# Fourier mixing and a gated MLP on one core: three reads of the first group issued by GpSimd, the last row's numbers of a piece of w_in by a transfer, and the last chunk's epilogue in smaller steps

## The chip, the cores and the metric

The kernel runs on one core of a Trainium2 chip. A core has five instruction streams: PE (matrix products; its weight loads are listed apart as PEld), DVE (VectorE), ACT (ScalarE), POOL (GpSimd) and SP (SyncE, which here only issues transfers). Each runs its own instructions in order and waits for the others by semaphores. Transfers are issued on the queues of SP, ACT or GpSimd. The metric is the device time of one execution in microseconds (us); lower is better.

## The reference

x has 8 batches of 3008 rows of 256 numbers, all float32. The reference takes the real part of a two-dimensional Fourier transform of each batch, and passes the 24064 rows through an MLP with a hard-swish gate:

```
X = real(fft(fft(x, axis=1), axis=2))      # (8, 3008, 256) -> (24064, 256)
h = X @ w_in                               # (24064, 2048)
g = h * clip(h + 3, 0, 6) / 6
out = g @ w_out                            # (24064, 256)
```

## The kernel before

**The mathematics.** The transform over 3008 = 47 x 64 rows is done in two stages of products with tables (`stage1`, `stage1_first` for the 47, `stage2` for the 64). The transform over the 256 columns is folded into w_in: the table C (256 x 256) times a piece of w_in gives the tile W1, so one product does both (`fold_w_in`, L664). The last of the 256 table rows is dealt with apart: its numbers, one for each of the 2048 columns of w_in, stand in row 127 of the second half of W1, and are needed spread over the partitions in the tile WN (128 x 16, one column for each block of 128 columns of w_in). DVE multiplies a column of WN with a row of data and adds it to a product (`s`, L401, in `activate`). The second matrix product of the MLP takes 7 block products in place of 8 (`mlp2`, L473), whose sums and differences are made in an epilogue (`finish`; for the last chunk of all `finish_final`, L513).

**Tiles and order.** Batches go in four pairs; a pair has 12 chunks of output frequencies in 6 groups of two; a chunk has 8 steps `fc`. A step takes blocks fc and fc + 8 of the 16 column blocks. In step fc of a chunk, `mlp1` makes two products u and v of W1 with the tile q of the group, `activate` makes the gate, `combine` three sums on GpSimd, and `mlp2` adds seven products into four PSUM tiles `acc`. The whole order is written out by hand: the tile framework places the semaphores, but moves nothing. The loop at L924 runs over the steps, with the next pair's stage 1 put beside them by due step. The first eight steps have an order of their own (`first_steps`, `second_steps`), since the weights are still being prepared.

**The start.** The first pair's x is read by GpSimd's queue, stage 1 runs column by column, and its result z is stored to DRAM by SP's queue (`zd`, L285). It comes back transposed as the tile g of the first group: `load_g(first, 0)` (L305), four reads on SP, two halves (`h`, L314) for two batches (`b`), which wait for the last store. Meanwhile the weights arrive in 16 pieces of 512 KB by GpSimd's queue (`load_w`, L577). Pieces 0 and 1 are the first two of w_in and 2 and 3 the first two of w_out. `see` (L743) is a copy of one column by GpSimd of the first half of g; it stands ahead of `load_w` for pieces 4 to 7 (L773), so these are issued only when the first half of g is there. Each piece is taken apart into exponent and mantissa and joined again (`exponent_a`, `exponent_b`, `exponent_c` at L605 to L625, `mantissa`, `join`). Then come `fold_w_in(0)` and `fold_w_in(1)` (L787, L791), `stage2` of the first group's first half (L797), and chunk 0's first products.

**fold_w_in.** Eight products on PE (16 instructions) into a PSUM tile, a copy of it into W1 by ACT (L684), and the numbers for WN. For piece 0 they go by two transfers on SP (L691), each from row 127 of W1, 128 numbers of 4 bytes, one to each partition. For piece 1 (`spread_by_pe=True`) PE multiplies instead the piece's own columns with the table's last row, four products of one column (L682, tile `pw`), and ACT copies the two columns into WN (L686). For later pieces a transfer is issued for the first of the two columns of each piece, and the second column of an even piece waits in the list `rest` until the next piece. The first step uses WN columns 0 (piece 0) and 8 (piece 1), the second step columns 1 and 9.

**The end.** In the last step of the last chunk `mlp2` makes its seven products in the order 0, 1, 2, 3, 4, 6, 5. After product 0 ACT copies it, scaled, into the tile e (L490). The other products are used from PSUM by DVE in `finish_final`: `add_product` adds a product to a sum (L522), `turn_both` transposes both halves of one output side together in 32 x 32 blocks (L526) and sends it in six stores (`send`, L555), which alternate between SP's queue and ACT's; in the second group of six the last one goes on SP. Four sums lead to the first side, `rn[:, 0]`; then two more, and one instruction for both halves of the second side (L537).

Of the kernel before, what the change touches and what calls it, by code (L numbers as in the profile page):

```python
# [7 lines left out]
F32 = mybir.dt.float32  # L8
# [5 lines left out]
AL = mybir.AluOpType  # L14
# [34 lines left out]
WS = 2.0 ** 20  # L49
# [9 lines left out]
def kernel(  # L59
# [10 lines left out]
    nc = tc.nc  # L70
    P = nc.NUM_PARTITIONS
    B, S, D = x.shape
    FF = moe_w_in.shape[1]
    NFC = FF // P
    NF = NFC // 2
# [12 lines left out]
    TB = KC * N2  # L88
    NH = N2 // 2 + 1
    NG = NCK // 2  # L90
    DH = 32
# [13 lines left out]
    ps_h = ctx.enter_context(tc.tile_pool(name="ps_h", bufs=3, space=PSUM))  # L105
# [14 lines left out]
    C = consts.tile([P, 2, D], F32, name="C")  # L120
    W1 = consts.tile([P, 2, FF], F32, name="W1")
    WN = consts.tile([P, NFC], F32, name="WN")
# [182 lines left out]
    def load_g(pr, gr):  # L305
        g = gpool.tile([P, 2 * KK, D + 1], F32, tag="g", name="g")
        gb = [g[b * N2:(b + 1) * N2] for b in range(2)]
        for b in range(2):
            zd = pr.zd[b, gr] if pr.p > 0 else pr.zd[gr, b]
            zd = zd.rearrange("k c n d -> (c n) k d")  # L310
            if pr.p > 0 or gr > 0:
                nc.sync.dma_start(out=gb[b][:, :, 0:D if pr.p > 0 else D + 1], in_=zd)

        for h in range(2 if pr.p + gr == 0 else 0):  # L314
            ks = slice(h * KK, (h + 1) * KK)
            for b in range(2):
                nc.sync.dma_start(out=gb[b][:, ks], in_=pr.zd[gr, b, ks].rearrange("k c n d -> (c n) k d"))
        for b in range(2) if pr.p > 0 else ():
            nc.sync.dma_start(out=gb[b][:, :, D], in_=pr.zq[gr, :, :, :, b].rearrange("k c n -> (c n) k"))
        pr.g[gr] = g  # L320
# [152 lines left out]
    def mlp2(ch, fc):  # L473
        a = ch.a.pop(fc)[:].rearrange("p m f n -> p (m f) n")[:, :, 0:ch.n]
        c = ch.c.pop(fc)
        moving = [a[:, 0], a[:, 1], a[:, 3], c[:, 0], c[:, 1], c[:, 2], c[:, 3]]
        order = list(enumerate(moving))
        if ch.final and fc == NF - 1:

            order[5:] = order[:4:-1]  # L480
        for i, mv in order:

            if fc == 0 and i % 2 == 0:
                ch.acc[i // 2] = ps_a.tile([P, 2, TB], F32, tag="acc", name="acc")
            nc.tensor.matmul(ch.acc[i // 2][:, i % 2, 0:ch.n], G[:, i, fc, :], mv,  # L485
                             start=(fc == 0 and i % 2 == 0), stop=(fc == NF - 1), skip_group_check=True)
            if ch.final:
                if fc == NF - 1 and i == 0:
                    ch.e = epool.tile([P, 8, TB], F32, tag="e", name="e")
                    nc.scalar.mul(ch.e[:, 0, 0:ch.n], ch.acc[0][:, 0, 0:ch.n], 1.0 / WS)  # L490
                continue
            if fc == NF - 1 and (i % 2 == 1 or i == 6):
                if i == 1:
                    ch.e = epool.tile([P, 8, TB], F32, tag="e", name="e")
                k = 2 * (i // 2)
                nc.scalar.mul(ch.e[:, k:i + 1, 0:ch.n], ch.acc[i // 2][:, 0:i + 1 - k, 0:ch.n], 1.0 / WS)  # L496

    def finish(ch):
# [14 lines left out]
    def finish_final(ch):  # L513
        n = ch.n
        e = ch.e[:, 0, 0:n]
        w = epool.tile([P, 3, TB], F32, tag="w", bufs=1, name="w")
        ch.r = epool.tile([P, 2, 2, TB], F32, tag="r", name="r")
        wn, rn = w[:, :, 0:n], ch.r[:, :, :, 0:n]
        os = [epool.tile([P, TB // DH, 2, DH], F32, tag="o", name="o") for m in range(2)]

        def add_product(out, i, in1, sign=1.0):
            nc.vector.scalar_tensor_tensor(out, ch.acc[i // 2][:, i % 2, 0:n], sign / WS, in1,  # L522
                                           op0=AL.mult, op1=AL.add)

        def turn_both(m):
            nc.vector.transpose(os[m][:, 0:n // DH].rearrange("p j h e -> p h j e"),  # L526
                                rn[:, m].rearrange("p h (j i) -> p h j i", i=DH))
            send(ch, os[m], m)

        add_product(rn[:, 0, 0], 1, e)  # L530
        add_product(wn[:, 0], 3, e)
        add_product(wn[:, 2], 6, wn[:, 0])
        add_product(rn[:, 0, 1], 5, wn[:, 2], -1.0)
        turn_both(0)
        add_product(wn[:, 1], 4, e)
        add_product(wn[:, 0], 5, wn[:, 1], -1.0)
        nc.vector.scalar_tensor_tensor(rn[:, 1], ch.acc[1][:, :, 0:n], 1.0 / WS, wn[:, 0:1].to_broadcast([P, 2, n]),  # L537
                                       op0=AL.mult, op1=AL.add)
        turn_both(1)

    def store(ch, m):
        o = epool.tile([P, TB // DH, 2, DH], F32, tag="o", name="o")
# [4 lines left out]
    def turn(ch, o, m, h):  # L547
        n = ch.n
        nc.vector.transpose(o[:, 0:n // DH, h], ch.r[:, m, h, 0:n].rearrange("p (j i) -> p j i", i=DH))  # L549

    def send(ch, o, m):

        queues = [nc.sync, nc.scalar, nc.sync, nc.scalar, nc.sync, (nc.scalar, nc.sync)[m]]
        for j, (bj, k1) in enumerate(ch.blocks[m]):
            (queues[j] if ch.final else nc.sync).dma_start(out=out_k[ch.pr.p, k1, bj], in_=o[:, j].rearrange("p h e -> p (h e)"))  # L555
# [105 lines left out]

    rest = []

    def fold_w_in(j, spread_by_pe=False):  # L664

        _, n, k = PIECES[j]
        nb = WB // 2
        cs = slice(in_column(n, k), in_column(n, k) + nb)
        wi = w.pop(PIECES[j]).rearrange("p (i f) -> p i f", i=2)

        ps = bank([P, 2, nb], "wps") if starting[0] else spare[k]
        for blk in range(2):
            for i in range(2):
                nc.tensor.matmul(ps[:, blk], C[:, i, blk * P:(blk + 1) * P], wi[:, i], start=(i == 0), stop=(i == 1))  # L674
        fs = range(cs.start // P, cs.stop // P)

        pw = None
        if spread_by_pe:
            pw = ps_h.tile([P, nb // P], F32, tag="uv", name="pw")
            for f in range(2):  # L680
                for i in range(2):
                    nc.tensor.matmul(pw[:, f:f + 1], wi[:, i, f * P:(f + 1) * P], C[:, i, D - 1:D],  # L682
                                     start=(i == 0), stop=(i == 1))
        nc.scalar.copy(W1[:, :, cs], ps[:])  # L684
        if pw is not None:
            nc.scalar.copy(WN[:, fs[0]:fs[-1] + 1], pw[:])  # L686
            return

        wait = [] if k or j == 0 else fs[1:]
        for f in [fs[0], *rest, *(() if wait else fs[1:])]:  # L690
            nc.sync.dma_start(out=WN[:, f:f + 1], in_=W1[P - 1:P, 1, f * P:(f + 1) * P])  # L691
        rest[:] = wait
# [95 lines left out]
    head_b(2)  # L788
    exponent_b(2)
    exponent_a(3)  # L790
    fold_w_in(1, spread_by_pe=True)  # L791
    head_b(3)
    exponent_b(3)
    tail(2)
# [54 lines left out]
    epool = None  # L849
# [7 lines left out]
    uv = mlp1_products(*chunk(0))  # L857
# [184 lines left out]
```

## Time and profile before

| | |
|---|---|
| device time, four runs | 1941.18, 1942.77, 1944.06, 1944.3 us (median 1943.42) |
| the profiled execution: device time, span | 1945.75 us, 1943.8 us |
| share of full clock granted to PE, mean | 0.997 |
| DVE, ACT, POOL busy | 1437.8, 680.6, 1417.6 us |
| read from and written to HBM | 57.57 MB, 37.32 MB |
| first product that is part of the second matrix product (L465) | 52.04 us |
| last product ends | 1934.4 us |

The span runs from the first instruction to the last of the profiled execution; the device time has also what lies around it. All times in the views count from the start of the span. In a line of the timeline the columns are the start, the length, the engine (a q after it: its queue of issued transfers), the line in the code, the operation, the tile written and those read, the number of merged instructions, and in brackets how long the engine had been idle and what ended that. A line of the chain has start, length, and the work or the transfer that the chain went through; "issue" is time in which the engine waited for nothing that the profile shows.

### The profile page before, as it was taken

The numbers are of one execution on the slowest core, as the hardware profiler recorded it, in microseconds if no ns is written. First come the engines' busy times: TensorE is split into PE (matmuls) and PEld (weight loads), VectorE is DVE, ScalarE is ACT, GpSimd is POOL, SyncE is SP. The second block draws the span as 40 slices with busy tenths as digits, with TensorE's granted clock in tenths as the row PEclk, the third lists the DMA queues.
The fourth block names the chain that finished last, engine by engine and source line by source line (L and its number), as shares of the span: only waits on it lengthen the run. The fifth ranks groups of instructions, "written<-read, shape, count | busy, mean of one in ns | idle before, by whom it ended". The sixth has DMA issues, their size and how long they took to land.

```text
span 1943.8 us, 27874 instructions
## 1 busy us (share of the span) xinstructions
PE 1926.7 (99%) x9228; PEld 1656.9 (85%) x9228; DVE 1437.8 (74%) x2777; ACT 680.6 (35%) x1162; POOL 1417.6 (73%) x1620
## 2 busy tenths in 40 slices
PE   9999999999999999999999999999999999999997
PEld 4578888888988888888898888888899888888887
DVE  6877777777777777777787777777778777777776
ACT  5633333333333333333333333333333333333332
POOL 4178888887678877787678877878666667666664
PEclk9999999999999999999999999999999999999999
DMA  8521222211111222111111221222110101101000
GB/s 225 189 72 47 74 49 55 55 44 31 39 33 50 57 74 55 44 50 32 37 36 46 55 55 44 50 53 52 35 28 20 28 17 28 34 12 28 21 18 20
DMA packets 149854, 96.70 MB, mean 50 GB/s; under 512 B 118687, under 2 KB 132131, under 8 KB 149710
## 3 DMA queue, kind: packets, MB, share of 16 engines
q1 hardware_dynamic: 138378, 58.09, 12.4%
q0 software_dynamic: 10672, 36.67, 6.5%
q8 instruction: 72, 1.18, 0.2%
q14 instruction: 72, 0.59, 0.1%
q10 hardware_dynamic: 660, 0.16, 0.0%
HBM read 57.57 MB, written 37.32 MB: 49 GB/s over the span
## 4 chain that ended last, share of the span: by engine, by line
PE 94%; DVE 2%; DMA 1%; ACT 1%; issue 1%; POOL 0%; DVEq 0%; ACTq 0%
PE acc L485 56%; PE v L392 16%; PE u L392 16%; PE ps L335 2%; PE acc L465 1%; PE ps L223 1%; DMA xt<-in_x_dram,IX 1%; DVE a L441 1%; DVE s L401 0%; ACT t L438 0%; DVE u L422 0%; PE spare L674 0%; PE ps L278 0%; DVE o L549 0%; DMA WN<-W 0%
## 5 line engine op out<-in xcount | busy, mean ns | idle before, releaser
L455 POOL TENSOR_TENSOR c<-a 128x512 f32<-128x512 f32 (+1 forms) x375 | 469.0, 1251 | 360.9 <-PE acc L485 291.9
L485 PE MATMUL acc<-c,G 128*128 128x256 f32 (+1 forms) x3008 | 696.9, 374 | 0.0
L438 ACT ACTIVATE t<-u,half 128x512 f32<-128x512 f32 (+1 forms) x384 | 260.8, 679 | 1141.3 <-DVE u L411 1056.0
L485 PEld LDWEIGHTS acc<-c,G 128*128 128x128 f32 x3008 | 565.4, 190 | 71.1
L401 DVE SCALAR_TENSOR_TENSOR s<-qn,WN,u 128x256 f32<-128x256 f32 (+1 forms) x768 | 330.5, 472 | 333.4 <-PE u L392 331.2
L485 PE MATMUL acc<-a,G 128*128 128x256 f32 (+1 forms) x2256 | 541.5, 375 | 0.5 <-ACT e L490 0.5
L485 PEld LDWEIGHTS acc<-a,G 128*128 128x128 f32 x2256 | 421.4, 190 | 71.9 <-issue 17.6
L392 PE MATMUL v<-q,W 127*128 127x256 f32 (+1 forms) x1536 | 389.3, 375 | 3.1 <-DVE a L441 3.1
L392 PE MATMUL u<-q,W 128*128 128x256 f32 (+1 forms) x1536 | 388.0, 375 | 0.3 <-ACT q L338 0.3
L441 DVE SCALAR_TENSOR_TENSOR a<-t,u 128x512 f32<-128x512 f32 (+2 forms) x448 | 263.9, 601 | 102.2 <-ACT t L438 98.5
L392 PEld LDWEIGHTS v<-q,W 127*128 127x128 f32 x1536 | 287.9, 190 | 43.8 <-DVE a L441 3.9
L392 PEld LDWEIGHTS u<-q,W 128*128 128x128 f32 x1536 | 285.7, 190 | 37.0 <-issue 1.9
L455 POOL TENSOR_TENSOR c<-a,c 128x256 f32<-128x256 f32 (+1 forms) x375 | 269.1, 717 | 29.4
L455 POOL TENSOR_TENSOR c<-c,a 128x256 f32<-128x256 f32 (+1 forms) x375 | 269.0, 717 | 29.4
L411 DVE TENSOR_TENSOR u<-s,v 128x512 f32<-128x512 f32 x352 | 245.0, 696 | 37.7 <-DVE s L401 1.4
L441 DVE SCALAR_TENSOR_TENSOR a<-t,v 128x512 f32<-128x512 f32 (+1 forms) x480 | 263.9, 567 | 0.3 <-ACT t L438 0.2
L438 ACT ACTIVATE t<-v,half 128x512 f32<-128x512 f32 (+1 forms) x384 | 260.7, 679 | 0.4 <-issue 0.2
L413 DVE TENSOR_TENSOR v<-v,s 128x512 f32<-128x512 f32 x352 | 244.0, 693 | 0.0
L455 POOL TENSOR_TENSOR r<-w,e 128x256 f32<-128x256 f32 (+1 forms) x92 | 88.8, 986 | 3.6
L496 ACT ACTIVATE e<-acc 128x512 f32<-128x512 f32 (+2 forms) x184 | 83.4, 545 | 0.0
L549 DVE STREAM_TRANSPOSE o<-r 128x256 f32<-128x256 f32 (+1 forms) x188 | 71.1, 417 | 0.1
L455 POOL TENSOR_TENSOR w<-w,e 128x512 f32<-128x512 f32 (+1 forms) x46 | 57.6, 1251 | 3.6
(113 smaller groups left out, 778.0 us busy)
## 6 DMA issues: line engine op xcount, KB each, us to landing
out_dram<-o SPq DMA_DIRECT2D x747, 32.0 KB
zd<-z SPq DMA_DIRECT2D x48, 192.0 KB
g<-zd SPq DMA_DIRECT2D x36, 256.0 KB
xt<-in_x_dram POOLq DMA_DIRECT2D x21, 256.0 KB, 3.7
qn<-qd SPq DMA_DIRECT2D x19, 256.0 KB
st<-in_moe_w_in_dram POOLq DMA_DIRECT2D x8, 512.0 KB, 4.6
st<-in_moe_w_out_dram POOLq DMA_DIRECT2D x8, 512.0 KB
xt<-in_x_dram POOLq DMA_DIRECT2D x17, 192.0 KB, 3.9
```

The costliest lines, as they stand in the source:

```text
L223: nc.tensor.matmul(ps[b][h * PB:(h + 1) * PB, 0:n], F[rows(b), 0:PB], y[rows(b), 2 * h:2 * h + n], start=True, stop=not last, skip_group_c ...
L335: nc.tensor.matmul(ps[:, blk, u * P:n].rearrange("p (b k) -> p b k", b=2), g[:, kk, blk * (P + 1):blk * (P + 1) + P], T[:, :, gr, blk, kk, ...
L392: nc.tensor.matmul(ps[:, i, 0:nq], W1[r, blk, f * P:(f + 1) * P], q[r, blk, of:of + nq], start=True, stop=True)
L401: nc.vector.scalar_tensor_tensor(s[:, i, 0:nq], qn[:, of:of + nq], WN[:, f:f + 1], u[:, i, 0:nq], op0=AL.mult, op1=AL.add)
L411: nc.vector.tensor_tensor(u[:], s[:], v[:], op=AL.add)
L413: nc.vector.tensor_tensor(v[:], v[:], s[:], op=AL.subtract)
L438: nc.scalar.activation(t, h, AF.Relu, bias=half[:], scale=scale)
L441: nc.vector.scalar_tensor_tensor(dst, t, 1.0, h, op0=AL.min, op1=AL.mult)
L455: (eng or nc.gpsimd).tensor_tensor(out, in0, in1, op=AL.add)
L485: nc.tensor.matmul(ch.acc[i // 2][:, i % 2, 0:ch.n], G[:, i, fc, :], mv, start=(fc == 0 and i % 2 == 0), stop=(fc == NF - 1), skip_group_c ...
L496: nc.scalar.mul(ch.e[:, k:i + 1, 0:ch.n], ch.acc[i // 2][:, 0:i + 1 - k, 0:ch.n], 1.0 / WS)
L549: nc.vector.transpose(o[:, 0:n // DH, h], ch.r[:, m, h, 0:n].rearrange("p (j i) -> p j i", i=DH))
```

## The change

Three parts, in one diff. In `load_g(first, 0)` the first of the four reads stays on SP, and the other three are issued by GpSimd. `fold_w_in` loses the way by PE: for piece 0 one transfer is issued and the other column waits in `rest`; for piece 1 three transfers follow its copy into W1: column 8, then column 1 (from `rest`), then column 9. In the last step of the last chunk ACT's copy of product 0 comes after product 1 in the order of the program, and `finish_final` transposes each half as soon as it is there (`turn`, L547, unchanged), with four smaller transposes in place of two, and two sums of one half in place of one instruction for both.

```
--- before.py
+++ after.py
@@ -314,7 +314,9 @@
         for h in range(2 if pr.p + gr == 0 else 0):
             ks = slice(h * KK, (h + 1) * KK)
             for b in range(2):
-                nc.sync.dma_start(out=gb[b][:, ks], in_=pr.zd[gr, b, ks].rearrange("k c n d -> (c n) k d"))
+
+                (nc.sync if h + b == 0 else nc.gpsimd).dma_start(
+                    out=gb[b][:, ks], in_=pr.zd[gr, b, ks].rearrange("k c n d -> (c n) k d"))
         for b in range(2) if pr.p > 0 else ():
             nc.sync.dma_start(out=gb[b][:, :, D], in_=pr.zq[gr, :, :, :, b].rearrange("k c n -> (c n) k"))
         pr.g[gr] = g
@@ -484,15 +486,14 @@
                 ch.acc[i // 2] = ps_a.tile([P, 2, TB], F32, tag="acc", name="acc")
             nc.tensor.matmul(ch.acc[i // 2][:, i % 2, 0:ch.n], G[:, i, fc, :], mv,
                              start=(fc == 0 and i % 2 == 0), stop=(fc == NF - 1), skip_group_check=True)
-            if ch.final:
-                if fc == NF - 1 and i == 0:
-                    ch.e = epool.tile([P, 8, TB], F32, tag="e", name="e")
-                    nc.scalar.mul(ch.e[:, 0, 0:ch.n], ch.acc[0][:, 0, 0:ch.n], 1.0 / WS)
-                continue
             if fc == NF - 1 and (i % 2 == 1 or i == 6):
                 if i == 1:
                     ch.e = epool.tile([P, 8, TB], F32, tag="e", name="e")
                 k = 2 * (i // 2)
+                if ch.final:
+                    if k == 0:
+                        nc.scalar.mul(ch.e[:, 0, 0:ch.n], ch.acc[0][:, 0, 0:ch.n], 1.0 / WS)
+                    continue
                 nc.scalar.mul(ch.e[:, k:i + 1, 0:ch.n], ch.acc[i // 2][:, 0:i + 1 - k, 0:ch.n], 1.0 / WS)
 
     def finish(ch):
@@ -522,21 +523,19 @@
             nc.vector.scalar_tensor_tensor(out, ch.acc[i // 2][:, i % 2, 0:n], sign / WS, in1,
                                            op0=AL.mult, op1=AL.add)
 
-        def turn_both(m):
-            nc.vector.transpose(os[m][:, 0:n // DH].rearrange("p j h e -> p h j e"),
-                                rn[:, m].rearrange("p h (j i) -> p h j i", i=DH))
-            send(ch, os[m], m)
-
         add_product(rn[:, 0, 0], 1, e)
+        turn(ch, os[0], 0, 0)
         add_product(wn[:, 0], 3, e)
         add_product(wn[:, 2], 6, wn[:, 0])
         add_product(rn[:, 0, 1], 5, wn[:, 2], -1.0)
-        turn_both(0)
+        turn(ch, os[0], 0, 1)
+        send(ch, os[0], 0)
         add_product(wn[:, 1], 4, e)
         add_product(wn[:, 0], 5, wn[:, 1], -1.0)
-        nc.vector.scalar_tensor_tensor(rn[:, 1], ch.acc[1][:, :, 0:n], 1.0 / WS, wn[:, 0:1].to_broadcast([P, 2, n]),
-                                       op0=AL.mult, op1=AL.add)
-        turn_both(1)
+        for h in range(2):
+            add_product(rn[:, 1, h], 2 + h, wn[:, 0])
+            turn(ch, os[1], 1, h)
+        send(ch, os[1], 1)
 
     def store(ch, m):
         o = epool.tile([P, TB // DH, 2, DH], F32, tag="o", name="o")
@@ -661,7 +660,7 @@
 
     rest = []
 
-    def fold_w_in(j, spread_by_pe=False):
+    def fold_w_in(j):
 
         _, n, k = PIECES[j]
         nb = WB // 2
@@ -673,20 +672,9 @@
             for i in range(2):
                 nc.tensor.matmul(ps[:, blk], C[:, i, blk * P:(blk + 1) * P], wi[:, i], start=(i == 0), stop=(i == 1))
         fs = range(cs.start // P, cs.stop // P)
-
-        pw = None
-        if spread_by_pe:
-            pw = ps_h.tile([P, nb // P], F32, tag="uv", name="pw")
-            for f in range(2):
-                for i in range(2):
-                    nc.tensor.matmul(pw[:, f:f + 1], wi[:, i, f * P:(f + 1) * P], C[:, i, D - 1:D],
-                                     start=(i == 0), stop=(i == 1))
         nc.scalar.copy(W1[:, :, cs], ps[:])
-        if pw is not None:
-            nc.scalar.copy(WN[:, fs[0]:fs[-1] + 1], pw[:])
-            return
-
-        wait = [] if k or j == 0 else fs[1:]
+
+        wait = [] if k else fs[1:]
         for f in [fs[0], *rest, *(() if wait else fs[1:])]:
             nc.sync.dma_start(out=WN[:, f:f + 1], in_=W1[P - 1:P, 1, f * P:(f + 1) * P])
         rest[:] = wait
@@ -788,7 +776,7 @@
     head_b(2)
     exponent_b(2)
     exponent_a(3)
-    fold_w_in(1, spread_by_pe=True)
+    fold_w_in(1)
     head_b(3)
     exponent_b(3)
     tail(2)
```

## The prediction

> **What bounds the kernel now.** I read the page first, then the chain of waits of the first 110 us, the timelines there engine by engine, the busy time by stretches, and the timeline of the last 20 us. The page settles where not to look:
>
> ```profile
> PE 1926.7 (99%) x9228; PEld 1656.9 (85%) x9228; DVE 1437.8 (74%) x2777; ACT 680.6 (35%) x1162; POOL 1417.6 (73%) x1620
> PE 94%; DVE 2%; DMA 1%; ACT 1%; issue 1%; POOL 0%; DVEq 0%; ACTq 0%
> ```
>
> PE is busy for 99% of the span and makes 94% of the chain. The diff touches no instruction between the second piece of w_in and the last chunk, so it can act in two places: before PE becomes gapless (about 76 us), where a shift of the start moves everything behind it one for one, and after the last product. The chain at the start:
>
> ```profile
> 44.05 0.80 PE pw L682 x8
> 44.85 0.02 issue
> 44.87 0.16 ACT WN L686
> 45.03 1.05 ACT ex L625 x2
> 46.08 0.48 ACT q L338
> ...
> 61.99 4.98 DMA WN<-W
> 66.98 0.02 issue
> 67.00 0.49 DVE s L401
> ```
>
> The reader is to see that PE's `pw`, its copy and ACT's next three instructions were on the chain, and that much later a `WN` transfer of one tile is waited for 4.98 us. GpSimd's timeline beside it:
>
> ```profile
> 44.70 0.62 POOL L744 COPY seen<-g 128x1 f32<-128x1 f32 x1 [14.65 <-DMA g<-zd]
> 45.26 1.44 POOL L585 DMA_DIRECT2D st<-in_moe_w_in_dram  x2
> ...
> 61.53 0.79 POOL L585 DMA_DIRECT2D st<-in_moe_w_in_dram  x1 [5.59 <-ACT PM L605]
> ```
>
> `see` holds GpSimd until the half-tiles of `g` are there (44.70); only then do the 512 KB reads of the next weight pieces start (45.26). The completions recorded in the trace put the four `g` reads, issued by SP at 40.95, 41.64, 42.29 and 42.94, at 43.62, 44.56, 45.07 and 45.77.
>
> **Part A, three g reads on GpSimd.** Removed: three issues of 0.60 to 0.64 us on SP. Added: three on GpSimd, which is idle from 30.05 to 44.70. Only the 256 KB and 512 KB direct reads show GpSimd's price, 0.54 to 0.78 us each; I take 0.6. The last store of `zd` lands at 40.75, SP issues at 40.95, so GpSimd issues at about 41.0, 41.6, 42.2. For landing the trace has no quiet GpSimd read of this size. Ends: SP's own 2.67 us for the first read, and 3.97 us for the 512 KB read issued at 45.26. I take 2.7, nearest in size: the second read is there at 43.7 instead of 44.56; by the other end it is 45.0, a loss of 0.4. `see` and the 512 KB reads then start about 0.85 earlier, the first of them at 44.4.
>
> On PE the gain is short, because PE finishes folding at 44.05 and ACT's copy of the second piece runs until 44.82. Without `pw` (0.80 on PE) and the 0.16 copy, ACT goes on with its two exponents; the second needs DVE's `ex`, done at 45.26, so it starts at 45.30, and the `q` copy at 45.79 instead of 45.98. Value of A and the removed `pw`: −0.2 us for `u`, whose first pair then ends at 47.55. Bounds −0.3 and +0.4.
>
> Of spreading reads over queues the row says that SP's issues were 0.60 to 0.64 us each. The Trainium skill ("DMA: Bandwidth & Descriptors", Rules for kernel authors) speaks against the change here: issuing from several engines does not help bandwidth, it only saves issue time. By that rule the second read would come 0.65 earlier, by my estimate from the rows 0.85; in either case `pw` and ACT leave the −0.2.
>
> **Part C, WN[:,8] by a transfer.** This is the term with the sign. Before, column 0 came by a transfer (issued 43.64, landed 45.94) and columns 8 and 9 by PE and ACT, ready at 45.03. Now column 8 waits for ACT's copy of the second piece (ends 44.82) and SP issues it at 44.87; columns 1 and 9 queue behind it on SP at about 45.4 and 46.0 and are first used at 56.2 and later, so they are hidden. DVE's first `s` (L401) starts after `u`, at 47.6; the second reads column 8 and would start at 48.0 (before: 48.24).
>
> How long does this transfer of 128 single numbers take? Quiet rows: issued 59.70, landed 61.24 (1.55); 78.92 to 80.87 (1.95). Rows with a GpSimd read in flight: 61.99 to 66.98 (4.98), 62.51 to 67.14 (4.63). The third line of the GpSimd view shows why I choose the second kind: that read was issued at 61.53, 0.46 ahead of the transfer; here, by part A, one is issued at 44.4, 0.47 ahead of it. Part A thus takes away the cover that `see` gave. I take the smaller of the two, 4.63, since here the stream has just begun: landed 49.5, second `s` at 49.52, which is **+1.28 us**. Bounds: quiet, 46.4 to 46.8, below what `u` allows, so −0.2; 4.98 gives +1.63.
>
> What is queued behind the waiting `s` on DVE: the adds, gates, the copies of q and qn, the mantissas of the next pieces. PE's `v` of the second chunk waits for the gate (0.26 idle at 51.07), ACT's relus for the adds, and the chain shows DVE, ACT and PE in turn from there to 61.99. I find no slack that takes up the shift, so it goes through whole. PE's extra idle of 1.3 us is near another cost:
>
> ```profile
> 67.60:71.00 3.40, 1.33 (x6) 1.06 (x6) 3.25 (x6) 2.69 (x5) 0.00 (x0) 1.00 0.90 325
> 71.05:74.46 3.41, 3.41 (x5) 1.35 (x4) 3.15 (x6) 2.18 (x4) 0.00 (x0) 0.50 1.02 412
> ```
>
> The columns to read are the length, PE busy, and the granted clock (the number after POOL's). In 3.40 us PE is idle for 2.07, and the next 3.41 us have clock 0.50; the same pair stands at 26.68 (1.77 idle) and 30.09. A halved stretch costs about 1.7 us of PE work. Idle of 0.26 + 1.28 = 1.54 at 51 us is below both rows that triggered it, so I add nothing, and keep +1.7 for the range. The Trainium skill ("TensorE: Matmul & The Clock Gate", HAM oscillation) puts the trouble at idle gaps above about 3.4 us, on a free-running window; the rows here show 2.07 in one gap to be enough, so the measurement decides, and by the page nothing would be added either.
>
> **Part B, the end.**
>
> ```profile
> 1931.85 0.33 ACT L490 ACTIVATE e<-acc 128x192 f32<-128x192 f32 x1 [3.01 <-PE acc L485]
> 1932.23 0.92 PE L485 MATMUL acc<-a,G 128*128 128x192 f32 x4 [0.48 <-ACT e L490]
> ...
> 1934.62 0.36 DVE L522 SCALAR_TENSOR_TENSOR r<-acc,w 128x192 f32<-128x192 f32 x1
> 1935.05 0.58 DVE L526 STREAM_TRANSPOSE o<-r 128x384 f32<-128x384 f32 x1
> ...
> 1935.66 4.13 ACTq L555 DMA_DIRECT2D out_dram<-o  x5
> ...
> 1936.30 0.56 DVE L537 SCALAR_TENSOR_TENSOR r<-acc,w 128x384 f32<-128x384 f32 x1
> 1936.89 0.58 DVE L526 STREAM_TRANSPOSE o<-r 128x384 f32<-128x384 f32 x1
> ```
>
> ACT's early copy of the first product did not run beside PE: PE's next product waits for it. Without the stall (rows: PE 1932.23, would be 1931.59 after two issues of 0.163 from 1931.26) PE ends 0.64 earlier. In the new order ACT waits for the second product: end 1932.08, copy 1932.17 to 1932.50, first add at 1932.54 (before 1932.86). From then DVE is the bound. Steps start to start: an add before a dependent instruction 0.39 (1935.91 to 1936.30), an add on the turned value 0.35; a turn of 192 columns is shown by the stores (0.334 alone) and I scale its step to 0.29 from 0.36 (256) and 0.50 (384). First turn 1932.93, adds 1933.22, 1933.62, 1934.01, second turn 1934.40 to 1934.74, plus 0.03: the first six stores are issued at 1934.80 instead of 1935.66, −0.86. After it: adds 1934.69, 1935.04, 1935.43; turn 1935.82; add 1936.11; turn 1936.50 to 1936.84, against 1937.47: −0.63. The two halves of the sum and turn cost 0.20 more than the joined ones, which the earlier start covers.
>
> What is late next is stores. SP stands idle from 1938.70 to 1939.55 for a semaphore that the ACT store of 1937.07 frees on landing (1939.53), and issues the last at 1940.13, landing 1942.73. This comes from the first six, so it moves by −0.86, as SP would be ready at 1938.1. Value −0.86; if the second six decide −0.63; if the copy still blocks PE, 0.
>
> **Sum.** Start +1.28, end −0.86: +0.4 us. The profiled execution has 1945.75 us around a span of 1943.8; the four timed runs have 1941.18 to 1944.3, median 1943.42, so it lies 2.3 above them, about what one halved stretch more gives. I put the difference on the median: **1943.8 us**.
>
> **Rivals.**
> 1. Column 8 lands quietly, because `g` comes no earlier from GpSimd or the small transfer passes ahead of the big one. For it: quiet rows of 1.55 to 1.95. Against: 61.99. Then −0.2 − 0.86: **1942.4**.
> 2. The end gives nothing, because the copy waits or the stores decide otherwise, and the start costs +1.28: **1944.7**. This covers also "the change doesn't do what it says": reads on GpSimd that land no earlier.
> 3. Slower than the bound: column 8 waits behind several of the six 512 KB reads, which keep the queues busy until 59.7. The worst small transfer, issued 63.16, landed 69.52 (6.4); from 44.87 that is 51.2, +3.0, PE idle 3.3 in one stretch, one stretch at half clock +1.7, and −0.86: **1947.3**. It decides from a landing at about 51.2 on.
>
> **Numbers.** Forecast 0.48, rival 1 0.25, rival 2 0.20, rival 3 0.07. A measurement of this kernel can tell about 0.2% (3.9 us) from no change. Only rival 3 reaches it, on its far half: slower 0.04; faster would take −3.9, which only two halved stretches lost together with rival 1 would give: 0.02; same 0.94. The range goes from rival 1 with its bound (1942.0) to rival 2 with part of a halved stretch more (1946.0).
>
> **What would show it.** A: `see` at about 43.9 and the next reads at 44.4; no `pw`. C: the second `s` of the first step apart from the first, waiting for `WN<-W`, until 49.5. PE's first `v` of the second chunk at 52.3. B: no wait of PE for `e`, first stores at 1934.8 less the shift, SP's last wait 0.86 earlier. I am wrong if `s` follows `s` at once, or if the first `s` of a later step takes up the shift.

## The result, and the profile after

The changed kernel took 1941.49 us (median of 34 runs, 1939.25 to 1945.68), the kernel before 1943.63 us beside it (55 runs, 1940.86 to 1948.6). The ratio is 0.999, with a 95% interval from 0.9985 to 0.9995: 1.0 to 2.9 us less. The forecast was 1943.8 us, 0.4 above the median of the four runs of before that were known then, in a range from 1942.0 to 1946.0. The difference lies within 0.2%, as the prediction thought most likely, but it has the other sign, and the time lies below the range. The profiled execution took 1942.24 us around a span of 1940.5 us.

The page looks as before; PE's busy time is 3.3 us shorter, 0.8 of which is `pw`:

```profile
PE 1923.4 (99%) x9220; PEld 1655.1 (85%) x9220; DVE 1438.5 (74%) x2780; ACT 680.4 (35%) x1161; POOL 1417.3 (73%) x1623
PE 94%; DVE 3%; DMA 1%; ACT 1%; issue 1%; POOL 0%; DVEq 0%; SPq 0%; ACTq 0%
```

The two places where the prediction saw a wait for WN stand in DVE's timeline of the changed kernel:

```profile
47.20 0.48 DVE L403 SCALAR_TENSOR_TENSOR s<-qn,WN,u 128x256 f32<-128x256 f32 x1 [0.88 <-PE u L394]
48.01 0.48 DVE L403 SCALAR_TENSOR_TENSOR s<-qn,WN,u 128x256 f32<-128x256 f32 x1 [0.33 <-DMA WN<-W]
...
65.37 0.87 DVE L403 SCALAR_TENSOR_TENSOR s<-qn,WN,u 128x256 f32<-128x256 f32 x2
```

The first two lines are step 0. The new wait for column 8 is there, but it moves the second `s` by 0.42, not by 1.28. The last line is step 2: its two `s` are merged into one line without a gap, so nothing waits for column 10. Before, 0.92 us of idle time stood between them. The stretches that were 67.60 to 71.00 and 71.05 to 74.46 before read now (length, PE, PEld, DVE, ACT, POOL, granted clock, DMA share, GB/s):

```profile
67.60:71.00 3.40, 2.47 (x8) 1.62 (x9) 3.25 (x7) 3.12 (x6) 0.00 (x0) 1.00 0.99 330
71.05:74.46 3.41, 3.41 (x13) 1.92 (x12) 3.12 (x7) 2.24 (x4) 0.00 (x0) 1.00 0.82 314
```

PE waits 1.06 us ahead of the `v` of step 3 instead of 2.07, and the clock stays at 1.00 where it was 0.50. The end, from the timeline of all engines:

```profile
1928.33 1.14 PE L487 MATMUL acc<-a,G 128*128 128x192 f32 x6
1929.24 0.33 ACT L495 ACTIVATE e<-acc 128x192 f32<-128x192 f32 x1 [3.06 <-PE acc L487]
...
1930.00 0.38 DVE L548 STREAM_TRANSPOSE o<-r 128x192 f32<-128x192 f32 x1
...
1931.99 2.67 ACTq L554 DMA_DIRECT2D out_dram<-o  x3
...
1933.69 0.38 DVE L548 STREAM_TRANSPOSE o<-r 128x192 f32<-128x192 f32 x1
```

ACT's copy now runs beside PE's next products, which no longer wait for it.

**Where the time went.** The start of the work differs between profiles of one kernel: the first fold product (tile `wps`) began anywhere from 37.2 to 41.8 us in the 13 profiles, and the four profiles of kernels whose edits can't reach it (before twice, the end alone, part C alone) already span 37.92 to 40.44. So I cut each profile at three marks: the first fold product, the first `u` product, and product 100 of `acc` (counted from 0), from where PE is gapless. From there to the 14th product from the end every profile took 1804.10 to 1804.14 us. For the profiled pair:

| stretch | before | after | difference |
|---|---|---|---|
| span's start to first fold product | 40.44 | 39.94 | −0.50 (scatter) |
| to first `u` | 6.17 | 6.02 | −0.15 |
| to product 100 of `acc` | 80.52 | 78.23 | −2.29 |
| to the 14th product from the end | 1804.13 | 1804.14 | 0.01 |
| to the last landing of a store | 11.47 | 10.72 | −0.75 |
| to the end of the span | 1.04 | 1.42 | +0.38 |

Most of it is in the third line, where the prediction had +1.28.

### The profile page after: what moved, and what is told of

The parts are those of the page before. It is cut to its first block, busy times and chain, and to the rows that moved or that the text cites. A ratio compares the mean times of both kernels' runs of the same rounds, so it can differ in the third digit from the quotient of the medians.

```text
span 1940.5 us, 27867 instructions
## 1 busy us (share of the span) xinstructions
PE 1923.4 (99%) x9220; PEld 1655.1 (85%) x9220; DVE 1438.5 (74%) x2780; ACT 680.4 (35%) x1161; POOL 1417.3 (73%) x1623
## 3 DMA queue, kind: packets, MB, share of 16 engines
q8 instruction: 72, 1.18, 0.2%
## 4 chain that ended last, share of the span: by engine, by line
PE 94%; DVE 3%; DMA 1%; ACT 1%; issue 1%; POOL 0%; DVEq 0%; SPq 0%; ACTq 0%
PE acc L487 56%; PE v L394 16%; PE u L394 16%; PE ps L337 2%; PE ps L223 1%; PE acc L467 1%; DVE a L443 1%; DMA xt<-in_x_dram,IX 1%; DVE s L403 0%; ACT t L440 0%; DVE o L548 0%; PE spare L673 0%; PE ps L278 0%; DVE u L424 0%; ACT PM L604 0%
```

## The experiments

Theory 1 is the prediction's reading: column 10 lands late because its transfer runs beside a 512 KB read by GpSimd, and no part of the change touches that. Theory 2 is the rival in the first expectations: the reads do make column 10 late, but the change, by part A, moves them and so takes the wait away. Theory 3 came out of the first four runs. The trace has a queue 8, kind "instruction", of 72 packets with 1.18 MB, 16 KB each; from one packet to the next PE has some 128 weight loads and as many products, so these seem to be PE's own instructions. Theory 3 says that such a packet, when it starts while a small WN transfer is under way, holds back the last of that transfer's 16 completions; and that `pw`, with eight weight loads and eight products, decided when the packet comes.

The queue table for the time from 62.5 to 64.6 of the kernel before, and from 61.7 to 65.6 of the changed one, that is, while column 10 is under way:

```profile
q8 instruction: 1, 0.02, 4.9%
```

```profile
q0 software_dynamic: 169, 0.63, 56.6%
q1 hardware_dynamic: 367, 0.00, 5.0%
```

Columns: packets, MB, share of the time of 16 engines. The packet of before took 4.9% of 16 x 2.1 us, 1.65 us in all. After, no q8 line is there: the packet came at 70.28 instead of 63.05.

All measurements in one table. "Block" is the start of queue 8's second packet, "lands" the last completion, both counted from the issue of column 10; "idle" is DVE's ahead of the second `s` of step 2 and PE's ahead of the `v` of step 3; "half" tells whether a stretch at clock 0.50 follows; "`u` to 100" is the third line of the table above.

| kernel | block | lands | DVE idle | PE idle | half | `u` to 100 | median us | ratio [95%] |
|---|---|---|---|---|---|---|---|---|
| before | 1.06 | 4.99 | 0.92 | 2.07 | yes | 80.52 | | |
| before_again | 1.00 | 4.27 | 0.19 | 1.35 | no | 78.09 | 1940.83 (one) | |
| a_only | 0.97 | 4.27 | 0.19 | 1.34 | no | 78.10 | 1943.38 | 0.9999 [0.999, 1.0008] |
| b_only | 1.09 | 5.37 | 1.29 | 2.46 | no | 79.21 | 1942.3 | 0.9994 [0.9985, 1.0003] |
| before_fill | 2.36 | 5.34 | 1.25 | 1.55 | no | 79.17 | 1942.99 | 0.9993 [0.9984, 1.0002] |
| after_pad | 1.12 | 5.13 | 1.05 | 2.21 | yes | 80.66 | 1943.89 | 1.0 [0.9991, 1.0009] |
| before_hold10 | 1.35 | 3.34 | 0 | 1.06 | no | 77.81 | 1942.17 | 0.9993 [0.9984, 1.0003] |
| before_more | 0.53 | 3.98 | 0 | 1.06 | no | 77.82 | 1942.62 | 0.999 [0.9981, 0.9999] |
| before_cut | 9.04 | 3.97 | 0 | 1.08 | no | 77.83 | 1942.88 | 0.9994 [0.9985, 1.0003] |
| ab_cut | 8.66 | 3.98 | 0 | 1.08 | no | 77.83 | 1941.65 | 0.9989 [0.998, 0.9998] |
| c_only | 8.65 | 3.88 | 0 | 1.07 | no | 78.95 | 1942.26 | 0.9993 [0.9984, 1.0002] |
| after | 8.52 | 3.83 | 0 | 1.06 | no | 78.23 | 1941.49 | 0.999 [0.9985, 0.9995] |
| after_again | 8.44 | 3.85 | 0 | 1.06 | no | 77.81 | 1941.8 | 0.9992 [0.9983, 1.0001] |

The column "`u` to 100" adds up: 77.82 where nothing waits for WN, plus the delay of the `s` that waits, plus 1.7 where a halved stretch follows. It is the sharpest instrument here, since the times scatter by about 4 us from run to run.

**a_only: part A alone.**

```
-                nc.sync.dma_start(out=gb[b][:, ks], in_=pr.zd[gr, b, ks]...)
+                (nc.sync if h + b == 0 else nc.gpsimd).dma_start(
+                    out=gb[b][:, ks], in_=pr.zd[gr, b, ks]...)
```

> The kernel before with part A alone: three of the four reads of the first g on GpSimd; columns 8 and 9 of WN still by PE, end unchanged. Theory 1 (the parts add: A is worth what u gains): u starts no earlier than pw and ACT allow, so 0 to -0.2 us. Rival (A moves the 512 KB weight reads ahead and with them, 16 us later, the wait for column 10 of WN, 4.98 us in the profile before and no wait in the profile after): 1 us or more faster, and the second s of step 2 starts right after the first.

GpSimd's timeline:

```profile
40.76 1.80 POOL L317 DMA_DIRECT2D g<-zd  x3 [9.69 <-DMA zd<-z]
44.32 0.35 POOL L745 COPY seen<-g 128x1 f32<-128x1 f32 x1 [1.75 <-DMA g<-zd]
```

SP issued its one read at 40.21, GpSimd its first at 40.76, 0.55 later, not together with it. `see` came 4.11 us after SP's issue; in the changed kernel 3.37 and 3.84, in the kernel before 3.75. Over all 13 profiles it came 3.59 to 4.68 us after it without part A (mean 4.08) and 3.37 to 4.11 with it (mean 3.69), so it is perhaps 0.4 earlier, half of what was forecast. The ratio is one, and first fold to first `u` is 6.22 beside 6.17 (before_hold10, before_more and before_fill, whose edits don't touch this stretch, took 6.44 to 6.50, for a cause that was not sought). At the start no gain of part A shows. Column 10 is still waited for, so theory 2 fails: part A doesn't take the wait away.

**b_only: part B alone.**

```
-                if fc == NF - 1 and i == 0:
+                if fc == NF - 1 and i == 1:
...
+        turn(ch, os[0], 0, 0)
...
-        turn_both(0)
+        turn(ch, os[0], 0, 1)
+        send(ch, os[0], 0)
...
-        turn_both(1)
+        for h in range(2):
+            add_product(rn[:, 1, h], 2 + h, wn[:, 0])
+            turn(ch, os[1], 1, h)
+        send(ch, os[1], 1)
```

> The kernel before with part B alone: ACT's copy after product 1, halves transposed one by one. Theory 1: PE does not wait for e, the first stores leave 0.74 us earlier against the last product's start than before (as the profile after shows), total -0.5 to -0.8 us. Rival (the end gives nothing since the last store decides on its own): 0.

Counted from the 14th product from the end, the last store lands 10.72 us later, before 11.47: −0.75, and the same to 0.02 in all five profiles with part B. The time can't tell −0.75 from nothing; the marks can. Its start is that of before, and there column 10 was later than in any other (5.37).

**c_only: part C alone.**

```
-        wait = [] if k or j == 0 else fs[1:]
+        wait = [] if k else fs[1:]
...
-    fold_w_in(1, spread_by_pe=True)
+    fold_w_in(1)
```

> The kernel before with part C alone: columns 8 and 9 of WN by transfers, all reads of g on SP. Theory 1: see still holds the 512 KB reads until after 44.6, so the transfer of column 8 (issued about 44.8) lands within 2.0 to 2.5 us, at about 47, and the second s follows the first without a wait: -0.2 us or nothing. If such a transfer takes 3.6 us also here, the contention with the weight reads is not what makes it long, and s waits about 0.3 us. Rival (SP is late, because four reads of g and two transfers stand ahead): lands after 48.3, +0.3 us or more.

DVE's timeline, step 0:

```profile
47.68 0.48 DVE L401 SCALAR_TENSOR_TENSOR s<-qn,WN,u 128x256 f32<-128x256 f32 x1 [1.03 <-DMA WN<-W]
```

Column 8 took 4.34 us from its issue at 43.31 and moved the `s` by 1.13, all of which is in "`u` to 100" (78.95). So the price of part C can be what the prediction said. What held it was not a read that `see` lets go: 15 of 16 completions came by 1.94, within what was expected, and the last alone came at 4.34, with queue 8's first packet starting at 44.04, 0.73 behind the issue. In the changed kernel that packet started 0.46 before the issue of column 8 (at 43.89), and no completion was left behind the others. All sixteen came between 2.85 and 3.63, as they do beside a 512 KB read, and GpSimd had issued one 0.50 ahead of the transfer of column 8 (issued at 44.35); in the second profile it was issued 0.04 ahead (44.34), and column 8 took 1.91 and nobody waited. The reads in the two profiles:

```profile
43.85 1.44 POOL L584 DMA_DIRECT2D st<-in_moe_w_in_dram  x2 [0.33 <-issue]
```

```profile
44.30 1.45 POOL L584 DMA_DIRECT2D st<-in_moe_w_in_dram  x2
```

At column 10, c_only is like the changed kernel: the block is far away and no one waits. Part C with `pw` removed can thus cost at one column and gain at another.

**before_hold10: GpSimd's read beside column 10 held back.** GpSimd copies one number of column 10 before it may issue its next read.

```
         if j in NEXT:
+            if j == 6:
+                see(WN[:, 10:11])
             load_w(NEXT[j])
```

> The kernel before with one copy more on GpSimd: it reads column 10 of WN ahead of the issue of the ninth weight read after see (load_w(12)), so that read starts only when the transfer of column 10 has landed. Theory 2 (the 4.98 us are contention with that read): the transfer lands within 2 us of its issue, the second s of step 2 does not wait, PE's idle time before v of chunk step 3 falls from 2.07 to about 1.1, too short for a halved stretch: 1 to 2.7 us faster in such runs, 1 to 2 us in the median. Rival (the long landing is not contention, or differs from run to run by chance): the transfer still takes 3 us or more now and then, median within 0.5 us of before.

GpSimd's line and DVE's `s` of step 2, in two views of this kernel:

```profile
64.44 0.29 POOL L746 COPY seen<-WN 128x1 f32<-128x1 f32 x1 [9.51 <-DMA WN<-W]
```

```profile
64.60 0.87 DVE L401 SCALAR_TENSOR_TENSOR s<-qn,WN,u 128x256 f32<-128x256 f32 x2
```

With no read in flight, 15 of the 16 completions came within 1.92 us of the issue, and the last at 3.34, with the block starting at 1.35. In the kernel before, 15 came by 3.69 and the last at 4.99. So there are two things: the 512 KB read costs all 16 some 1.8 us, and something else holds back one of them by another 1.3 to 1.4. An `s` can start without delay when column 10 lands within about 4.0 us; the read alone would be free, and only the last sixteenth made the wait. This run led to theory 3.

**before_cut and ab_cut: fewer PE instructions, `pw` kept.** Four products that only keep PE awake, and that nothing uses, are left out of stage 1; ab_cut has parts A and B besides.

```
-        if k < NXC - 1:
+        if 3 < k < NXC - 1:
             keep_awake(1)
```

> The kernel before with four of the seven single awake products between the first columns of stage 1 left out (they compute nothing that is used): 8 weight loads and 8 matmuls fewer on PE, the same number that the change takes away with pw, and pw itself is kept. Theory 3: queue 8 brings a 16 KB block of PE's instructions once in 256 of them on one DMA engine, and in the kernel before that block (63.05) falls on the transfer of column 10 of WN. With 8 pairs fewer it comes some 7 us later, near 70; column 10 lands within 4.0 us of its issue, the second s of step 2 does not wait, PE's idle before v is about 1.1 instead of 2.1 to 2.5. From wps to the steady part 83.98 us instead of 84.98 to 85.34 plus 1.7 per halved stretch; 1 to 2.5 us faster than before in the median. Rival (the length of that transfer is the weight reads' doing or chance): landing 4.3 to 5.4 as in before, a_only and b_only, same time.

> Parts A and B without C (columns 8 and 9 by PE), and four awake products left out as in before_cut. If theory 3 and the sums by stage hold: no wait for column 8 (0.27 us better than the changed kernel), no wait for column 10, the end as in the changed kernel: 0 to 0.3 us faster than the changed kernel, 2 to 2.5 us faster than before. Rival (C itself is what helps): as b_only.

The block moves to 70.26 and 70.24, all completions are there by 3.97 and 3.98, and the wait and the long PE idle go, without part C. In time before_cut shows little of it, 0.3 us by the medians where 1 to 2.5 were expected. It had two stretches at clock 0.50 in a row from 22.70 on (6.8 us; ab_cut from 23.51) where those products were missing, so the edit has a price of its own, and its time alone is inconclusive. ab_cut, which does without part C, stands at 1941.65, beside 1941.49 and 1941.8 for the changed kernel: no version better than the changed kernel was found.

**after_pad: the changed kernel with as many PE instructions as `pw` had.** One of the opening awake products becomes five products of one column that nothing uses.

```
-    keep_awake(9)
+    keep_awake(8)
+    small = ps_h.tile([P, 2 * TB], F32, tag="uv", name="small")
+    for i in range(5):
+        nc.tensor.matmul(small[:, i:i + 1], ones[:], Z[:, 0:1], start=True, stop=True)
```

> The changed kernel with one of the nine first awake products replaced by five of one column: 8 weight loads and 8 matmuls more on PE ahead of everything, in the same time. Theory 3: PE's instruction block comes back to about 63, column 10 lands 4.3 to 5.4 us after its issue, the second s of step 2 waits 0.2 to 1.4 us, PE's idle before v is 1.3 to 2.5 with the halved stretch in some runs; the block near 44 is gone too, so column 8 may land earlier. 1 to 2.5 us slower than the changed kernel, about the median of before less the end's 0.7. Rival (the changed order of transfers is what helps): as the changed kernel, 1941.5.

DVE's second `s` of step 2, and two stretches of 3.41 us:

```profile
63.82 0.48 DVE L403 SCALAR_TENSOR_TENSOR s<-qn,WN,u 128x256 f32<-128x256 f32 x1 [1.05 <-DMA WN<-W]
```

```profile
63.87:67.28 3.41, 1.20 (x6) 0.75 (x5) 3.15 (x6) 2.14 (x4) 0.00 (x0) 1.00 0.93 303
67.28:70.69 3.41, 3.41 (x7) 1.69 (x6) 3.20 (x6) 2.16 (x5) 0.00 (x0) 0.50 1.01 408
```

Everything that the change had removed is back: the block 1.12 us behind the issue, 15 completions by 3.89 and the last at 5.13, a wait of 1.05, PE idle 2.21, the halved stretch. Parts A, B and C are all in place, and the time is that of before (ratio 1.0). By the medians it is 2.1 above the unpadded kernel run beside it (1941.8, after_again), by the means 1.7; the two sets of eleven runs overlap. This is the run that speaks most clearly for theory 3, with one profile.

**after_again: the changed kernel, unaltered.**

> The changed kernel once more, for a second profile and as a yardstick on this chip. Theory 3: PE's block again near 44 and 70, column 10 lands within 4.0 us, no second halved stretch. If the short landing was chance: column 10 over 4.0 us and a wait.

Nothing waits for WN at all (77.81), neither for column 8 nor for column 10: `s` follows `s` at once, which the prediction named as a sign that it is wrong. The block that was expected near 44 came at 40.94, before the transfer of column 8.

**before_more: the kernel before with more work for PE.**

```
     keep_awake(9)
+    small = ps_h.tile([P, 2 * TB], F32, tag="uv", name="small")
+    for i in range(4):
+        nc.tensor.matmul(small[:, i:i + 1], ones[:], Z[:, 0:1], start=True, stop=True)
```

> The kernel before with PE work added: behind its opening keep_awake(9) stand four more one-column products that nothing uses, as many PE instructions as pw has. Theory 3 (a 16 KB block of PE's instructions, fetched by queue 8 about 1 us after column 10's transfer is issued, holds back its last sixteenth): the block that stood at 63.05 comes some 6 to 8 us earlier (55 to 58), before that transfer is issued; column 10 lands 3.8 to 4.0 after its issue, the second s of step 2 waits for nothing, PE idles some 1.1 before v of step 3, and no halved stretch follows. From the first fold product to the 100th acc product 84.0 to 84.2 (before: 86.69, before with GpSimd's read held back: 84.27). Time 0.9 to 2.6 below the kernel before, although it has more work. Theory 1 (the wait for column 10 comes from the 512 KB reads alone): column 10 lands as late as before, 4.3 to 5.4, and the time is the same within 0.3. What would fall between: the earlier block meets the transfer of column 2, issued near 59.7, which then lands late.

PE's timeline:

```profile
70.40 1.13 PE L392 MATMUL v<-q,W 127*128 127x256 f32 x4 [1.06 <-DVE a L441]
```

No wait, no halved stretch, 77.82, and 1.45 us less by the medians (the interval is 0.2 to 3.7), although PE has more to do. The place of the block was missed, though: it came only about half a microsecond earlier against the issue (0.53; 6 to 8 earlier was expected), took 0.98 us, and was over at 1.51. That it was over too early to hold back a completion is argued, not shown: in c_only the packet beside column 8 was over at 1.65, and the last completion came at 4.34. By theory 1 column 10 would have been late as before.

**before_fill: PE work laid into the stall.** The products of the first half of `u` and `v` of step 3 are made twice, the second time over the first.

```
-                nc.tensor.matmul(ps[:, i, 0:nq], W1[r, blk, ...], q[r, blk, ...],
-                                 start=True, stop=True)
+                for _ in range(1 + (more if blk == 0 else 0)):
+                    nc.tensor.matmul(ps[:, i, 0:nq], W1[r, blk, ...], q[r, blk, ...],
+                                     start=True, stop=True)
...
-        activate(*chunk(s + 1), *(mlp1_products(*chunk(s + 1)) if s > 0 else uv))
+        activate(*chunk(s + 1), *(mlp1_products(*chunk(s + 1), more=1 if s == 2 else 0) if s > 0 else uv))
```

> The kernel before, with each product of the first of the two halves of u and v of step 3 made twice (start=True, so the numbers stay the same): some 0.5 to 1 us of PE work laid into the stall before v of step 3. The place of the blocks of instructions ahead of it isn't moved. Theory 3: column 10's transfer still meets the block near 63 and lands 4.3 to 5.4 after its issue, the second s of step 2 waits 0.3 to 1.4; but PE's idle time before v of step 3 is 0.5 to 1 shorter than the 2.07 of before, so that no halved stretch follows. If the halved stretch is what most of the loss was, 84.9 to 85.4 from the first fold product to the 100th acc product, plus the 0 to 0.6 that the doubled products cost; time 0 to 1.7 below before. Rival: the halved stretch belongs to a longer count of PE's work than this one idle, and stands near 71 again: 86.7 or more, time the same or up to 0.6 above.

DVE and PE:

```profile
66.58 0.48 DVE L402 SCALAR_TENSOR_TENSOR s<-qn,WN,u 128x256 f32<-128x256 f32 x1 [1.25 <-DMA WN<-W]
```

```profile
69.36 1.13 PE L393 MATMUL v<-q,W 127*128 127x256 f32 x4 [1.55 <-DVE a L442]
```

The straggler and the wait are there, the stall is 1.55 instead of 2.46 (b_only, with the same wait), and no halved stretch follows. But none followed in b_only either, with 2.46, so this run agrees with the theory and, taken alone, doesn't prove that the shorter stall prevented it. Why b_only had none is told under "What stays open".

**before_again: a second profile of the kernel before.**

> The kernel before, unchanged, for a second profile. Theory 3: the block of PE's instructions starts 0.9 to 1.4 after column 10's transfer is issued, 15 of 16 of its completions come by 3.9 and the last at 4.2 to 5.4; the second s of step 2 waits 0.2 to 1.4. If it waits over 0.9, PE idles over 2.0 before v of step 3, and a halved stretch near 71 is possible, not certain. Theory 1: no tie to the block; if column 10 lands under 4.0 with the block in that place, theory 3 has a gap.

```profile
63.76 0.48 DVE L401 SCALAR_TENSOR_TENSOR s<-qn,WN,u 128x256 f32<-128x256 f32 x1 [0.19 <-DMA WN<-W]
```

The block is at 1.00, the straggler at 4.27, the wait small and no halved stretch. So the pair of profiles in the section above overstates the change: the first profile of before had a bad draw of both.

## Why the prediction was wrong

**The step that failed is part C, with its "here the stream has just begun: landed 49.5 ... +1.28".** The duration of 4.63 us came from two rows, 61.99 and 62.51, that were read as "Rows with a GpSimd read in flight". They also had a block of PE's instructions in flight, and the last part of their length goes with the block: 15 of 16 completions of the first came by 3.69. What the read does was forecast rightly and sized too large. In the changed kernel it was issued 0.50 ahead of column 8 (forecast 0.47), all sixteen completions were late, and column 8 took 3.63 and cost 0.42, a third of the term. In its second profile the read was 0.04 ahead, and column 8 took 1.91 and cost nothing. (The quiet row of 1.55 is the first of its sixteen completions; the last came at 1.90.) Where a block fell on it, in c_only, it took 4.34 and cost 1.13, near the prediction's term, for another reason. The profile's page named queue 8 with its 72 packets; I never asked when they came.

**The second half of the same step: "I find no slack that takes up the shift, so it goes through whole".** This is true of column 8's shift: c_only's 1.13 and the changed kernel's 0.42 come through whole. But the wait for column 10, 4.98 in the chain, was carried along as if it belonged to the program. It hung on where a block of PE's instructions fell, which `pw` helps to decide: part C's removal of 0.80 us of PE's work was priced by its time alone (−0.2, measured −0.15), not by what the removed instructions do to the place of everything fetched later. Without them, or with as many others left out (before_cut, ab_cut), the delay of 1.0 at column 10 goes, and with it the halved stretch that had followed PE's 2.07 us of idle time. Over the profiles whose start is that of before or of part A (before, before_again, a_only, b_only) "`u` to 100" is 78.98 in the mean, over the two of the changed kernel 78.02: −1.0 where the prediction had +1.28. With four profiles and two, this mean hangs on how many of them have a halved stretch.

**The halved stretch was in the text and not in the sum.** The prediction noted that its profile lay 2.3 above the median and that one halved stretch more would give that. It then put the difference on the median as if both executions were alike, and kept 1.7 only as a risk of the change. It was a loss that before sometimes has: one of its two profiles shows it. The granted clock of the timed runs agrees: it is 0.9977 in the mean of 86 runs of before, 0.9981 in 47 of the changed kernel and 0.9978 in the 11 of after_pad. A halved stretch takes 0.0009 off this mean (half of 3.41 us in 1941), so before had about 0.4 more of them in a run, by estimate 0.6 us. The difference is 2.3 times its standard error, and the mean doesn't tell where in the span the stretches stood.

**Part A: "the second read is there at 43.7 ... `see` and the 512 KB reads then start about 0.85 earlier".** GpSimd issues 0.55 after SP, not with it, and `see` came on average 0.4 us earlier after SP's issue than without part A, with a scatter of as much. None of it shows in first fold to first `u`, which the prediction expected too, since PE and ACT cover it.

**Part B: right in its mechanism, sized a little too large.** PE no longer waits for `e`. From the 14th product from the end, the first six stores are issued at 3.66 instead of 4.40 (−0.74, forecast −0.86), the last turn ends at 5.73 instead of 6.21 (−0.48, forecast −0.63), the last store lands at 10.72 instead of 11.47 (−0.75). The mis-sized terms are two adds, 0.43 and 0.46 from start to start where 0.40 and 0.39 were taken, and the turn of 192 columns: 0.38, where the stores' 0.334 was taken. (The prediction's own terms end at 1934.77, not at the 1934.80 that it used.) It is the first six stores that decide, as the prediction had it. Of the 0.75, the span of the changed kernel keeps 0.37; this is told below.

**The whole.** The means of the parts, −0.15 ahead of `u`, −1.0 from there to product 100, −0.75 at the last landing and +0.2 net behind it, give about −1.7, inside the measured −1.0 to −2.9. Of the rivals, the first (column 8 lands quietly, 1942.4) came nearest and is what the second profile of the changed kernel shows; it too kept the wait for column 10. Part C must be valued as a whole: in these profiles it cost 0 to 1.1 at column 8 and removed 0.3 to 2.7 at column 10 and behind it.

**What stays open.** That the block and the late sixteenth share one DMA engine is argued from the one late completion; the views give no engine for a packet. What sets the moment of a block isn't settled: before_more moved it by half a microsecond and the same number of instructions less by some eight, and the first block stood 1.7 to 2.0 ahead of the first fold product or 0.8 to 5.1 behind it.

Whether a halved stretch follows seems to depend on where PE's idle time falls. In each of the 13 profiles the changes of the clock lie whole multiples of 3.413 us apart, so the windows can be counted on from the first change. The idle time ahead of the `v` of step 3 lay in one window in before (2.07) and after_pad (2.21), and the next window was halved. In b_only the 2.46 us fell across two windows, 0.73 and 1.73 (behind each window stand its length and PE's busy time), and no halved one followed:

```profile
63.27:66.68 3.41, 2.69 (x11) 1.28 (x9) 2.01 (x4) 0.80 (x2) 1.21 (x2) 1.00 0.88 210
66.68:70.10 3.42, 1.69 (x6) 1.25 (x7) 3.27 (x6) 3.15 (x6) 0.00 (x0) 1.00 1.03 353
70.10:73.51 3.41, 3.41 (x11) 1.57 (x10) 3.15 (x7) 1.92 (x4) 0.00 (x0) 1.00 0.95 365
```

In before_fill the 1.55 us lay in one window. Without the doubled products some 2.4 us would have stood there, an estimate from b_only's 2.46 with the same wait, so the shorter stall probably did prevent a halved stretch. The idle time in one window isn't the whole rule, though: between 19 and 29 us, windows with 1.29 to 1.83 us of it came before a halved one, and two with 1.32 did not. The Trainium skill ("TensorE: Matmul & The Clock Gate", HAM oscillation) asks for gaps above about 3.4 us; the runs show 2.07 within one window to be enough.

## What to carry to other kernels

Before a wait for a transfer is carried through a change as fixed, ask what else was in flight when it was measured, instruction queues included, and look whether all parts of the transfer were late or only one. Removing or adding a few instructions on a long program moves every later instruction fetch, so an edit can pay or cost far from its place; a padding run with as many idle instructions tells this apart from the edit itself. And when the one profiled run lies above the median, look for the accident in it first, and leave it out of what the change is measured against.

## What the runs showed of the hardware

- **An instruction fetch goes with a late end of a small transfer.** At column 10, a 16 KB packet of queue 8 that starts 1.0 to 2.4 us behind the issue of a transfer of 128 numbers goes with its last completion coming 0.3 to 1.5 us behind the other fifteen (seven profiles: before, before_again, a_only, b_only, before_fill, before_hold10, after_pad); at 0.53, or far away, there is no such straggler (six profiles). Among all 190 WN transfers of the 13 profiles, twelve have their last completion over 0.9 us behind the fifteenth. In eleven of them such a packet started 0.58 to 2.35 us behind the issue; the twelfth (c_only, issued at 62.58, 1.49 behind) has none near, so something else can do it too. The Trainium skill ("Runtime: NRT & Kernel Launch", Instruction fetch mechanics) says that an engine's sequencer fetches 16 KiB blocks of 256 instructions over a DMA queue of its own, and calls the cost mostly hidden. The size and the count agree with the trace; the cost here is not to the engine that fetches, but to a transfer beside it.
- **A transfer of 128 single numbers** landed in 1.91 us quietly, and in 3.63 to 3.98 us beside a 512 KB read on GpSimd's queue when no block of instructions held back its last completion.
- **Part A lengthens the last steps of the program.** In the profiles with part A the span ends 1.42 to 1.54 us after the last landing, in the others 0.92 to 1.05. Between two of GpSimd's last instructions, a drain and a semaphore, stand 0.39 us instead of 0.09. The time around the span is some 0.2 shorter in the same kernels (means over their timed runs 1.77 to 1.86; others 1.97 to 2.09). GpSimd's stream is six instructions longer; whether this is a fetch too was not tested.
